# Three instructions moved in the hand-written order of a fused S4D and bilinear-GLU kernel

## The chip, the cores and the metric

The kernel runs on one core of a Trainium2 chip. A core has a matrix engine (TensorE, PE in the profile, with its weight loads listed apart as PEld), a vector engine (VectorE, DVE), a scalar engine (ScalarE, ACT), GpSimd (POOL) and SyncE (SP). Each engine works through its own list of instructions strictly in order, and the engines meet through semaphores. Matrix results stand in PSUM, from which DVE or ACT copies them away; SP and POOL issue the DMAs here. The metric is the device time of one execution in microseconds. A change of about 1% is what the measurement of this kernel can tell from none.

## What is computed

Two branches share one output and are mixed by a gate. Branch A is a state-space convolution: a kernel K of 2048 taps for each of 512 channels is built from complex exponentials, and the input is convolved with it by FFT. Branch B is a bilinear feed-forward layer.

```python
# A: S4D convolution, L = 2048, D = 512, N = 128
P = jnp.exp((A * dt[:, None])[:, :, None] * pos[None, None, :])
K = 2.0 * jnp.einsum("dn,dnl->dl", C, P).real
y = jnp.fft.irfft(jnp.fft.rfft(u_t, L2) * jnp.fft.rfft(K, L2)[None], L2)[:, :, :L]
a = y.transpose(0, 2, 1) + u * D_skip[None, None, :]
# B: bilinear GLU, F = 1792
b = jnp.einsum("bsf,fd->bsd", (x @ w_gate) * (x @ w_up), w_down)
# the mix
g = sigmoid((u * gate_w).sum(-1, keepdims=True))
out = g * a + (1 - g) * b
```

## The kernel before

**Branch B** (`glu`, line 820) holds most of the matrix work. The 14 tiles of F stand in four groups of 3, 3, 4 and 4, and for each group the four chunks of 512 tokens are passed. `hidden` (line 726) forms `pg` and `pu` for one tile of F, each from 12 matmuls of 512 columns: every float32 product is split into a high and a low part and taken as three matmuls. ACT copies `pg` into `h`, DVE multiplies by `pu`, ACT casts the high part `hh`, and DVE subtracts for the low part `hl`. `down` (line 753) multiplies `hh` and `hl` with the down weights and sums over the group in a PSUM bank `y`, one for each 128 tokens. There are two banks `y`, so the third of a chunk waits until the first has been copied away. `evacuate` (line 764) does that: an ACT activation `acc<-y,ngate` scales by 1 - g, and a DMA issued by POOL adds `acc` to the output in memory. `acc` has three buffers.

**Branch A** builds its tables on DVE and ACT. `v_table` (line 1165) makes the table `v` for one of 16 blocks of the state, by an outer product and then twice by squaring: ACT squares the real part into `v` and the imaginary part into `sq`, DVE forms twice the product (`SCALAR_TENSOR_TENSOR v<-v`) and subtracts (`TENSOR_TENSOR v<-v,sq`). The first squaring has 16 columns, the second 8 and reads the first. `k_block` (line 1206) multiplies the tables `x` and `v` on PE into a bank `k`, which ACT and DVE bring into `kt`. Every fourth block a quarter of the channels is complete and goes through the transform: `k_first` (line 1240), then four times `m_second` (line 1325: 32-row matmuls into four banks `k`, copied by ACT into `ev`), `m_product` (line 1351: complex product of the spectra on DVE, `y<-ev`, `ev<-ev`, twice `y<-y,ev`), twice `m_inverse` (line 1382: back into four banks `k`, copied by ACT into `ts`, written to memory `y_d`), and `m_last`. There are four banks `k`.

**The order.** All this is recorded as tasks, numbered as they are added. `Work.plan` (line 357) sets an order for each engine by a planner with estimated durations. Then `Work.run` (line 455) applies a table of numbers, `AHEAD` (line 446): a pair (n, m) takes task n out of its engine's line and puts it directly ahead of task m. After that the instructions are issued in this order, engine by engine; an engine never leaves its order. The lines of the page read L126 for all of them, since one helper, `InOrder`, records every operation; so groups are told apart by the names of their tiles.

```python
for n, other in self.AHEAD:
    line = lines[at[n].engine]
    line.remove(at[n])
    line.insert(line.index(at[other]), at[n])
```

Of the kernel before, what the change touches and what calls it, by code (L numbers as in the profile page):

```python
# [206 lines left out]
class Work:  # L207
# [149 lines left out]
    def plan(self):  # L357
# [95 lines left out]
    )  # L453

# [1163 lines left out]
```

## Time and profile before

| | |
|---|---|
| Median of 3 runs | 584.13 us (579.15, 584.13, 584.96) |
| The profiled execution | 578.89 us, of which the span from first to last instruction is 577.1 us |
| DVE busy | 509.9 us (88%) |
| ACT busy | 400.9 us (69%) |
| POOL busy | 113.6 us (20%) |
| DMA | 136.28 MB moved, mean 236 GB/s |
| Granted TensorE clock | 1.000 of full speed over the span |

Of a timeline's row the columns are: start in us from the span's beginning, duration in us, engine, line, operation, out<-in, shapes, count, and in brackets the idle time of the engine before it with what ended it. Rows of equal instructions that follow each other are merged, with their count behind an x. Ends of matmuls are modelled. An engine's next instruction can start some hundredths of a microsecond before the end of the one ahead of it.

### The profile page before, as it was taken

The numbers are of one execution on the slowest core, as the hardware profiler recorded it, in microseconds if no ns is written. First come the engines' busy times: TensorE is split into PE (matmuls) and PEld (weight loads), VectorE is DVE, ScalarE is ACT, GpSimd is POOL, SyncE is SP. The second block draws the span as 40 slices with busy tenths as digits, with TensorE's granted clock in tenths as the row PEclk, the third lists the DMA queues.
The fourth block names the chain that finished last, engine by engine and source line by source line (L and its number), as shares of the span: only waits on it lengthen the run. The fifth ranks groups of instructions, "written<-read, shape, count | busy, mean of one in ns | idle before, by whom it ended". The sixth has DMA issues, their size and how long they took to land.

```text
span 577.1 us, 14851 instructions
## 1 busy us (share of the span) xinstructions
PE 571.2 (99%) x6006; PEld 435.4 (75%) x6006; DVE 509.9 (88%) x812; ACT 400.9 (69%) x891; POOL 113.6 (20%) x159
## 2 busy tenths in 40 slices
PE   8999999999999999999999999999999999999997
PEld 7777777888886877788677868876878786776775
DVE  6999999999998989999999999997999996247555
ACT  5459888997588499967896775799877534243351
POOL 0003222412010240311122401102333103111011
PEclk9999999999999999999999999999999999999999
DMA  8999969998665798989779857978989349798976
GB/s 277 403 348 371 415 223 348 272 231 241 126 178 141 273 231 186 253 204 285 201 219 245 197 134 246 220 186 210 304 138 297 71 167 255 243 294 235 289 160 127
DMA packets 71687, 136.28 MB, mean 236 GB/s; under 512 B 6852, under 2 KB 35780, under 8 KB 69188
## 3 DMA queue, kind: packets, MB, share of 16 engines
q1 hardware_dynamic: 47668, 87.10, 43.8%
q0 software_dynamic: 23392, 47.98, 39.8%
q8 instruction: 47, 0.77, 0.5%
q10 hardware_dynamic: 560, 0.26, 0.2%
q14 instruction: 20, 0.16, 0.1%
HBM read 80.27 MB, written 55.05 MB: 234 GB/s over the span
## 4 chain that ended last, share of the span: by engine, by line
PE 79%; DVE 13%; ACT 4%; DMA 2%; issue 2%; DVEq 0%
PE y L126 23%; PE pg L126 22%; PE pu L126 22%; PE k L126 12%; DVE v L126 3%; DVE x L126 2%; DMA raw<-in_wts 2%; DVE h L126 1%; DVE y L126 1%; DVE hl L126 1%; DVE m L126 1%; DMA y<-in_xT 1%; ACT ev L126 1%; DVE ev L126 1%; DVE t L126 1%
## 5 line engine op out<-in xcount | busy, mean ns | idle before, releaser
L126 PE MATMUL pg<-xs,whi 128*128 128x512 f32 x448 | 138.6, 390 | 0.5 <-ACT whi L126 0.5
L126 PE MATMUL pu<-xs,whi 128*128 128x512 f32 x448 | 138.1, 389 | 0.0
L126 PEld LDWEIGHTS pg<-xs,whi 128*128 128x128 f32 x448 | 84.0, 188 | 18.3 <-ACT whi L126 0.7
L126 PEld LDWEIGHTS pu<-xs,whi 128*128 128x128 f32 x448 | 84.1, 188 | 17.1
L126 PE MATMUL y<-dhi,hl 128*128 128x512 f32 x224 | 90.3, 403 | 0.3 <-ACT acc L126 0.2
L126 PE MATMUL pg<-xs,wlo 128*128 128x512 f32 x224 | 89.3, 399 | 0.0
L126 PE MATMUL pu<-xs,wlo 128*128 128x512 f32 x224 | 89.0, 397 | 0.0
L126 PE MATMUL y<-dlo,hh 128*128 128x512 f32 x224 | 87.4, 390 | 0.0
L126 PE MATMUL y<-dhi,hh 128*128 128x512 f32 x224 | 87.2, 389 | 0.0
L126 POOL DMA_DIRECT2D out<-acc x44 | 38.7, 938 | 168.7 <-ACT acc L126 168.3
L126 ACT COPY ev<-k 128x512 f32<-128x512 f32 x112 | 59.5, 599 | 14.0 <-PE k L126 11.3
L126 ACT CAST hh<-h 128x512 fp32r<-128x512 f32 x56 | 34.7, 620 | 46.4 <-DVE h L126 46.1
L126 DVE TENSOR_TENSOR h<-pu,h 128x512 f32<-128x512 f32 x56 | 38.5, 687 | 23.2 <-PE pu L126 20.8
L126 ACT ACTIVATE acc<-y,ngate 128x512 f32<-128x512 f32 x62 | 41.9, 688 | 24.0 <-PE y L126 22.2
L126 PEld LDWEIGHTS y<-dhi,hl 128*128 128x128 f32 x224 | 42.0, 187 | 21.5 <-issue 7.8
L126 PEld LDWEIGHTS pg<-xs,wlo 128*128 128x128 f32 x224 | 42.0, 188 | 18.4 <-issue 9.2
L126 PEld LDWEIGHTS pu<-xs,wlo 128*128 128x128 f32 x224 | 42.0, 188 | 15.7 <-issue 6.1
L126 ACT COPY h<-pg 128x512 f32<-128x512 f32 x56 | 33.0, 590 | 28.4 <-PE pg L126 22.5
L126 PEld LDWEIGHTS y<-dhi,hh 128*128 128x128 f32 x224 | 42.1, 188 | 9.0
L126 PEld LDWEIGHTS y<-dlo,hh 128*128 128x128 f32 x224 | 42.1, 188 | 7.8
L126 DVE TENSOR_TENSOR hl<-h,hh 128x512 fp32r<-128x512 f32 x56 | 38.5, 688 | 5.4 <-ACT hh L126 4.8
L126 DVE TENSOR_TENSOR v<-m,v 128x896 f32<-128x896 f32 x32 | 34.1, 1085 | 0.2
(134 smaller groups left out, 961.3 us busy)
## 6 DMA issues: line engine op xcount, KB each, us to landing
xs<-xs_d SPq DMA_DIRECT2D x36, 512.0 KB, 6.2
out<-acc POOLq DMA_DIRECT2D x44, 256.0 KB, 6.5
raw<-in_wts SPq DMA_DIRECT2D x33, 256.0 KB, 4.7
xs_d<-xs SPq DMA_DIRECT2D x16, 512.0 KB, 7.8
su_d<-ev POOLq DMA_DIRECT2D x32, 256.0 KB, 6.1
y_d<-ts SPq DMA_DIRECT2D x28, 256.0 KB, 5.6
in<-su_d POOLq DMA_DIRECT2D x12, 512.0 KB, 8.0
sk_d<-ev SPq DMA_DIRECT2D x6, 1024.0 KB, 3.9
```

The source lines that it names most:

```text
L126: got = getattr(self.engine, name)(*args, **kw)
```

## The change

Three pairs are added to the table. Nothing else is changed: no instruction is added or taken away, and the lists of PE, SP and POOL stay as they were.

```diff
         (2111, 1052), (2112, 2204), (2225, 2204), (2108, 2113), (2110, 2113), (1054, 2114),
+        (939, 1905), (2326, 2178), (1260, 2182),
         (2168, 1223), (2307, 1226), (2320, 1226), (2169, 1227), (2170, 1227),
```

The first pair, (939, 1905), moves the copy of the last `y` of a chunk in the third group on ACT. In the list of before it stands between a copy of `pg` into `h` and a load of an activation table; `t` and `rt` are phases, `x`, `kt` and `v` pieces of the tables of branch A.

```order
L126 COPY h<-pg 128x512
L126 ACTIVATE acc<-y,ngate 128x512
L126 ACT_TABLE_LOAD
L126 ACTIVATE t<-t 128x672
L126 COPY x<-pb 128x64
L126 COPY kt<-k 128x8x2x16
L126 ACTIVATE rt<-rt,fixed 128x672
L126 COPY v<-ri 128x32x4
L126 COPY v<-ri 128x32x7
L126 COPY v<-ri 128x32x4
L126 COPY v<-ri 128x32x7
L126 CAST hh<-h 128x512
```

The same stretch of ACT's list now:

```order
L126 COPY h<-pg 128x512
L126 ACT_TABLE_LOAD
L126 ACTIVATE t<-t 128x672
L126 COPY x<-pb 128x64
L126 COPY kt<-k 128x8x2x16
L126 ACTIVATE rt<-rt,fixed 128x672
L126 COPY v<-ri 128x32x4
L126 COPY v<-ri 128x32x7
L126 COPY v<-ri 128x32x4
L126 COPY v<-ri 128x32x7
L126 CAST hh<-h 128x512
L126 ACTIVATE acc<-y,ngate 128x512
```

The copy into `acc` stands ten instructions later, behind the cast of `h` into `hh` and ahead of the copies of `k` into `ts`. The DMA that adds this `acc` to the output keeps its place in POOL's list and waits for the copy.

The second pair, (2326, 2178), is on DVE, in the last quarter of the kernel, where the last block's `v` is squared beside the spectral product (`y` and `ev`) of the third quarter of the channels.

```order
 L126 TENSOR_TENSOR y<-ev 128x1024
 L126 SCALAR_TENSOR_TENSOR v<-v 128x32x16
-L126 TENSOR_TENSOR ev<-ev 128x2x2x256
-L126 TENSOR_TENSOR v<-v,sq 128x32x16
+L126 TENSOR_TENSOR v<-v,sq 128x32x16
+L126 TENSOR_TENSOR ev<-ev 128x2x2x256
 L126 TENSOR_TENSOR y<-y,ev 128x512
 L126 SCALAR_TENSOR_TENSOR v<-v 128x32x8
```

The end of the first squaring of `v` has changed places with the second half of the product.

The third pair, (1260, 2182), is on ACT at the same time of the program, behind the second squaring of `v`.

```order
 L126 ACTIVATE v<-v 128x32x8
 L126 ACTIVATE sq<-v 128x32x8
-L126 COPY ev<-k 128x2x2x128
-L126 ACTIVATE acc<-y,ngate 128x512 x2
+L126 ACTIVATE acc<-y,ngate 128x512
+L126 COPY ev<-k 128x2x2x128
+L126 ACTIVATE acc<-y,ngate 128x512
 L126 COPY ev<-k 128x2x2x128 x3
 L126 COPY kt<-k 128x8x2x16
```

The first of two copies into `acc` has changed places with the first of four copies of `k` into `ev`.

## The prediction

> **What bounds the kernel now.** I read the page first: busy times and the chain of work that ended last.
>
> ```profile
> span 577.1 us, 14851 instructions
> ...
> PE 571.2 (99%) x6006; PEld 435.4 (75%) x6006; DVE 509.9 (88%) x812; ACT 400.9 (69%) x891; POOL 113.6 (20%) x159
> ...
> PE 79%; DVE 13%; ACT 4%; DMA 2%; issue 2%; DVEq 0%
> ```
>
> PE holds 79% of the chain and is busy for 99% of the span. A move on another engine can therefore only shorten the time where PE stands still for that engine. The second view is the list of waits, PE alone; its columns are the total, the number and the longest, in us.
>
> ```profile
> PE k L126 <- DVE acc L126: 1.1, 1, 1.1
> PE pg L126 <- ACT whi L126: 0.5, 1, 0.5
> PE y L126 <- ACT acc L126: 0.2, 1, 0.2
> ```
>
> That is all PE waits for in this execution: 1.8 us. The first two lie at the start (the warm-up's zeroes and the first weights). The third is a matmul into `y` that waits for ACT to copy an older `y` into `acc`, and this is the operation that two of the three moves shift. So I looked for that wait in the timelines. PE:
>
> ```profile
> 477.87 0.39 PE L126 MATMUL y<-dhi,hh 128*128 128x512 f32 x1
> ...
> 479.02 0.61 PE L126 MATMUL pg<-xs,whi 128*128 128x512 f32 x2
> 479.80 0.50 PE L126 MATMUL y<-dhi,hl 128*128 128x512 f32 x1 [0.16 <-ACT acc L126]
> 480.14 0.40 PE L126 MATMUL y<-dlo,hh 128*128 128x512 f32 x1
> 480.38 0.40 PE L126 MATMUL y<-dhi,hh 128*128 128x512 f32 x1
> 480.70 1.99 PE L126 MATMUL k<-v,x 128*32 128x64 f32 x128
> ...
> 486.94 2.00 PE L126 MATMUL k<-kt,w1k_t 32*128 32x512 f32 x16
> ```
>
> The matmul at 479.80 is the first of the chunk's third `y` and needs the bank of the first `y`, whose last matmul is that at 477.87. ACT and DVE at the same time:
>
> ```profile
> 475.14 0.64 ACT L126 ACTIVATE sq<-v 128x512 f32<-128x512 f32 x1
> 477.79 0.69 ACT L126 ACTIVATE v<-v 128x256 f32<-128x256 f32 x1 [2.01 <-DVE v L126]
> 478.26 0.43 ACT L126 ACTIVATE sq<-v 128x256 f32<-128x256 f32 x1
> 478.59 0.56 ACT L126 COPY ev<-k 128x512 f32<-128x512 f32 x1
> 479.06 1.26 ACT L126 ACTIVATE acc<-y,ngate 128x512 f32<-128x512 f32 x2
> 480.21 1.56 ACT L126 COPY ev<-k 128x512 f32<-128x512 f32 x3
> ```
>
> ```profile
> 475.32 0.68 DVE L126 SCALAR_TENSOR_TENSOR v<-v 128x512 f32<-128x512 f32 x1
> 475.92 1.21 DVE L126 TENSOR_TENSOR ev<-ev 128x1024 f32<-128x1024 f32 x1
> 477.06 0.69 DVE L126 TENSOR_TENSOR v<-v,sq 128x512 f32<-128x512 f32 x1
> ...
> 481.80 1.23 DVE L126 TENSOR_TENSOR y<-ev 128x1024 f32<-128x1024 f32 x1 [1.86 <-ACT ev L126]
> ...
> 486.07 0.26 DVE L126 TENSOR_TENSOR kt<-kt,skip 128x64 f32<-128x64 f32 x1
> ```
>
> ACT waits 2.01 us for DVE's `v<-v,sq` at 477.06, then squares, copies one `ev`, and only at 479.06 begins the `acc` that PE needs. It ends at 479.06 + 0.69 = 479.75 (one `acc` is 688 ns in the page), and PE starts at 479.80.
>
> **Moves two and three, the late `acc`.** What the wait costs: the two `pg` matmuls at 479.02 take 0.61 together and one alone 0.39, so the step from one to the next is 0.61 - 0.39 = 0.22 to 0.23. The next was due at 479.02 + 0.23 + 0.23 = 479.48 and came at 479.80: 0.32 late. The step behind it is 480.14 - 479.80 = 0.34 where 0.23 is usual: 0.11 more. The cost is 0.43 us.
>
> [...] The rows show steps of 0.22 to 0.24 us with nothing waiting, so the sum goes by the rows.
>
> Move two puts `v<-v,sq` at 475.92, in the place of `ev<-ev`. Its `sq` is ready at 475.14 + 0.64 = 475.78, and DVE is free at 475.92, so it doesn't wait. It ends at 476.61; ACT, which started 0.04 after DVE's end before (477.06 + 0.69 = 477.75, then 477.79), squares from 476.65 and is done at about 477.5, 1.14 earlier. `ev<-ev` then runs from 476.52 to 477.73 and the next product starts where `v<-v,sq` ended before. For the rest of DVE the two only change places: cost nothing.
>
> Move three lets `acc` start as soon as ACT is free and the first `y` is ready. How soon that is shows where ACT waited for PE, elsewhere in the trace:
>
> ```profile
> 364.54 0.39 PE L126 MATMUL y<-dhi,hh 128*128 128x512 f32 x1
> ```
>
> ```profile
> 364.97 0.69 ACT L126 ACTIVATE acc<-y,ngate 128x512 f32<-128x512 f32 x1 [0.26 <-PE y L126]
> ```
>
> That is 0.43 after the last matmul's start, so here 477.87 + 0.43 = 478.30. With both moves `acc` runs from 478.30 to 478.99, and PE may go on at 479.04, 0.44 ahead of its due time 479.48. The wait is gone: -0.43 us. The two moves are each enough alone. With move three alone `acc` takes the place of `ev` at 478.59, ends at 479.28, and PE is free at 479.33. With move two alone `ev` comes first, but at about 477.5, and `acc` again starts at 478.30. Their gains do not add.
>
> What pays: the first `ev` copy now starts behind `acc`, at 478.30 + 0.59 = 478.89 in place of 478.59, and ends at about 479.45. Its bank is the first that `k<-v,x` can take, which moves to 480.27: 0.8 to spare. The four `ev` copies end at about 481.5, no later than the 481.77 of before, so DVE's `y<-ev` is no later either. What is late next: `k<-kt` on PE moves from 486.94 to 486.51. It needs DVE's `kt<-kt,skip`, which ends at 486.33 even if DVE gains nothing. That leaves 0.18, so the gain passes here too. Bounds: 0 (another wait takes it up) and -0.43; I take -0.43, since each follower quoted has room.
>
> **Move one.** Its place, on ACT and then on DVE:
>
> ```profile
> 328.92 0.70 ACT L126 ACTIVATE acc<-y,ngate 128x512 f32<-128x512 f32 x1
> ...
> 334.03 0.62 ACT L126 CAST hh<-h 128x512 fp32r<-128x512 f32 x1
> 337.32 0.59 ACT L126 COPY ts<-k 128x512 f32<-128x512 f32 x1 [2.67 <-PE k L126]
> ```
>
> ```profile
> 333.31 0.69 DVE L126 TENSOR_TENSOR h<-pu,h 128x512 f32<-128x512 f32 x1
> ```
>
> All from the table load to the copies into `v` starts up to 0.6 earlier. But `hh` needs DVE's `h`, ready at 333.31 + 0.69 = 334.00, and started at 334.03. So `hh` gains nothing, and the 0.6 becomes idle time ahead of it. `acc` then runs from about 334.55 to 335.25, in the 2.67 us in which ACT waits for PE. PE has no wait within 10 us of this place, so nothing there can be gained: 0. What it might cost is the bank `y` and the store, both 5.6 us later:
>
> ```profile
> 348.82 0.39 PE L126 MATMUL y<-dhi,hl 128*128 128x512 f32 x1
> ```
>
> ```profile
> 356.91 1.72 POOL L126 DMA_DIRECT2D out<-acc  x2 [26.09 <-ACT acc L126]
> ```
>
> The next `y` is asked for at 348.82, 13 us after the copy ends. POOL has been idle for 26 us when it issues its next DMA, so nothing is queued behind the later store. Cost 0; the bounds are 0 and the 3.3 us of the second rival.
>
> **The sum.** 0 - 0.43 = -0.43 us: span 576.7, and 578.46 against the 578.89 of the profiled execution, or -0.07%. The runs shown lie in two places, 579.15 beside the profiled 578.89, and 584.13 and 584.96; the median of three, 584.13, is in the upper. A gain of 0.43 does not move runs from one to the other, so I put the new median at 584.13 - 0.43 = 583.7.
>
> **Rivals.** *No gain.* PE is not the true bound, or a wait behind the place takes the 0.43 back. For it: the 0.18 of `k<-kt`, and DVE's 13% of the chain. Against it: no PE wait is listed behind 479.80. [...] Time: 578.89, median 584.1.
>
> *Slower by the late store.* The `acc` of move one now is sent at about 335.3 and meets the writes of `y_d` and the loads behind them on SP's queue:
>
> ```profile
> 339.36 2.72 SPq L126 DMA_DIRECT2D y_d<-ts  x4
> ...
> 348.17 0.50 SPq L126 DMA_DIRECT2D in<-y_d  x1
> 348.71 1.54 SPq L126 DMA_DIRECT2D xs<-xs_d  x3
> ```
>
> ```profile
> xs<-xs_d SPq DMA_DIRECT2D x4, 512.0 KB, 8.8
> ...
> y_d<-ts SPq DMA_DIRECT2D x4, 256.0 KB, 3.0
> ```
>
> ```profile
> DMA to landing us min/median/max: 4.0/6.3/12.1
> ```
>
> ```profile
> 364.77 0.39 PE L126 MATMUL pg<-xs,wlo 128*128 128x512 f32 x1
> ```
>
> The last of the three rows of landings is that of `acc`. `y_d` lands at about 342.08 + 3.0 = 345.1, 3.1 ahead of `in<-y_d`. The last `xs` lands at about 350.25 + 8.8 = 359.1, 5.7 ahead of PE's use of it. It decides from a delay of 3.1 + 5.7 = 8.8 us. If the store's longest landing, 12.1, came on top in full, PE would wait 12.1 - 8.8 = 3.3 us: 582.2 for the profiled execution and 587.4 for the median. Against it: at the usual 6.3 the store is through before `y_d` is half written.
>
> *Faster by the runs' spread.* If the 5.2 us between the two places where runs lie are waits at one of the three moved instructions, the median falls to 578.5. For it: nothing in the trace, which is of the quicker kind. Against it: three moves of 0.6 us each.
>
> **How the numbers follow.** The forecast has 0.60, no gain 0.25, the late store 0.05, the spread 0.10. The predicted time is 583.7. The range goes from 578.0, the lower place with the gain and 0.5 for the scatter within a place, to 585.8, the highest run and as much again as the two upper runs differ (0.83). About 1% of 584.13 is 5.8 us, what a measurement can tell from none: below 578.3 or above 590. Faster takes half of the spread's case (its 578.5 lies on the edge) and 0.07 for a median that falls to the lower place by chance: 0.12. Slower takes the late store when it is worse than priced, and as much for chance: 0.05. The rest, 0.83, is no change.
>
> **What would show it.** Right: at about 479.5 PE goes from `pg` to `y` without a wait for `acc`, ACT's second squaring starts near 476.6, `acc` near 478.3, and `k<-kt` comes some 0.4 earlier. Move one: `acc` near 334.6, idle time ahead of `hh`, and PE as before up to 365. Wrong: a new PE wait behind 480, or `xs` late at 365.

## The result and the profile after

Beside each other, in 14 executions each:

| kernel | median us | lowest to highest |
|---|---|---|
| before | 582.26 | 578.83 to 585.75 |
| after | 578.77 | 578.17 to 579.61 |

The ratio is 0.9939, with a 95% interval of 0.9916 to 0.9961: 0.6% faster. The whole interval lies below 1, but the step is smaller than the 1% that counts as a change for this kernel, so the two count as the same. The lower ends differ by 0.7 us, the upper ends by 6.1 us. The change has made the time of the quick executions of before the usual one. The forecast was 583.7 us, and no change: the verdict came true, the time lies within the range of 578.0 to 585.8, and the median is 4.9 us off.

The profiled execution of after took 579.12 us, against 578.89 of before, though the median fell by 3.5 us. The profile of before is thus one of its quick executions, and a comparison of the two profiled executions shows no gain. The page of after:

```profile
span 577.3 us, 14851 instructions
...
PE 571.8 (99%) x6006; PEld 436.1 (76%) x6006; DVE 510.3 (88%) x812; ACT 400.8 (69%) x891; POOL 113.4 (20%) x159
...
PE 98%; DMA 1%; ACT 0%; DVE 0%; issue 0%; DVEq 0%
```

The chain that ended last is now PE for 98%, where it was PE for 79%. The list of waits of PE in after (total, number, longest) has only the two of the start left:

```profile
PE k L126 <- DVE acc L126: 1.1, 1, 1.1
PE pg L126 <- ACT whi L126: 0.5, 1, 0.5
```

The place of moves two and three, in the timelines of after (start, duration, both us, then the instruction; the idle time ahead of it in brackets). PE:

```profile
479.65 0.62 PE L126 MATMUL pg<-xs,whi 128*128 128x512 f32 x2
480.11 0.39 PE L126 MATMUL y<-dhi,hl 128*128 128x512 f32 x1
480.33 0.39 PE L126 MATMUL y<-dlo,hh 128*128 128x512 f32 x1
480.56 0.39 PE L126 MATMUL y<-dhi,hh 128*128 128x512 f32 x1
481.03 1.99 PE L126 MATMUL k<-v,x 128*32 128x64 f32 x128
...
487.30 2.00 PE L126 MATMUL k<-kt,w1k_t 32*128 32x512 f32 x16
```

From the pair of `pg` to the first `y` PE takes 480.11 - 479.65 = 0.46 us, where it took 0.78, and from there to the next 0.22, where it took 0.34: 0.44 us gained, and the forecast had 0.43. Behind it, `k<-v,x` starts 0.47 after the matmul ahead of it; in before that step was 0.32. So 0.15 is given back. DVE in after shows why:

```profile
477.08 0.91 DVE L126 TENSOR_TENSOR v<-v,sq 128x512 f32<-128x512 f32 x1
477.87 1.25 DVE L126 TENSOR_TENSOR ev<-ev 128x1024 f32<-128x1024 f32 x1
...
480.23 0.66 DVE L126 TENSOR_TENSOR v<-v,sq 128x256 f32<-128x256 f32 x1
```

The second `v<-v,sq` writes what `k<-v,x` reads and ends at 480.89, while PE was due at 480.56 + 0.32 = 480.88 and began at 481.03. ACT in after, at the place of move one and then at that of move three:

```profile
328.79 0.59 ACT L126 COPY h<-pg 128x512 f32<-128x512 f32 x1 [0.19 <-PE pg L126]
329.39 1.28 ACT L126 ACT_TABLE_LOAD   x1
...
334.38 0.62 ACT L126 CAST hh<-h 128x512 fp32r<-128x512 f32 x1 [0.33 <-DVE h L126]
334.90 0.68 ACT L126 ACTIVATE acc<-y,ngate 128x512 f32<-128x512 f32 x1
337.67 0.59 ACT L126 COPY ts<-k 128x512 f32<-128x512 f32 x1 [2.08 <-PE k L126]
...
478.94 0.69 ACT L126 ACTIVATE acc<-y,ngate 128x512 f32<-128x512 f32 x1
479.52 0.58 ACT L126 COPY ev<-k 128x512 f32<-128x512 f32 x1
```

Both copies into `acc` stand where the prediction put them: the first at 334.90 (334.55 was forecast, and the place as a whole comes 0.35 later here), the second at 478.94, which is 0.71 before the pair of `pg`, as forecast (479.02 - 478.30 = 0.72). The steps are right, then, and yet they sum to 0.3 to 0.4 us where the median fell by 3.5. The rest must come from something that the profile of before does not show as a wait.

### The profile page after: what moved, and what is told of

It reads as the page before. It is cut to its first block, busy times and chain, and to the rows that moved or that the text cites. A ratio compares the mean times of both kernels' runs of the same rounds, so it can differ in the third digit from the quotient of the medians.

```text
span 577.3 us, 14851 instructions
## 1 busy us (share of the span) xinstructions
PE 571.8 (99%) x6006; PEld 436.1 (76%) x6006; DVE 510.3 (88%) x812; ACT 400.8 (69%) x891; POOL 113.4 (20%) x159
## 4 chain that ended last, share of the span: by engine, by line
PE 98%; DMA 1%; ACT 0%; DVE 0%; issue 0%; DVEq 0%
PE y L126 28%; PE pg L126 27%; PE pu L126 27%; PE k L126 15%; DMA y<-in_xT 1%; ACT acc L126 0%; ACT xs L126 0%; DVE kt L126 0%; DVEq L1613 0%; ACT whi L126 0%
```

## The experiments

Two theories stood at the start. **The late store**: `acc` has three buffers, so the copy of move one needs the buffer whose store is the first of POOL's three `out<-acc` just ahead. Where POOL is late, that store lands late, ACT stands still at the copy, and everything behind it on ACT is late; move one takes the copy out of that place. **Moves two and three**: the wait at 479.80 is longer in most executions than in the profiled one, and its removal is the gain. The profile of before allows the first. POOL's timeline of before:

```profile
302.61 1.58 POOL L126 DMA_DIRECT2D out<-ts  x1 [2.60 <-ACT x L126]
310.34 1.56 POOL L126 DMA_DIRECT2D out<-ts  x1 [6.15 <-ACT ev L126]
...
321.37 2.75 POOL L126 DMA_DIRECT2D out<-acc  x3
```

and its transfers in the stretch that holds the first of those three alone (count, KB each, us from issue to landing):

```profile
out<-acc POOLq DMA_DIRECT2D x1, 256.0 KB, 7.4
```

The store lands at 321.37 + 7.4 = 328.8, and ACT's copy starts at 328.92: it made it by 0.15 us, and so left no wait.

**Move one alone, moves two and three alone, before once more, and an earlier store.** The rows left in the table of the change were

```diff
+        (939, 1905),
```

> Only the first pair, (939, 1905), is added to the table of before. Theory S (late store): in most runs of before POOL sends the first of three stores out<-acc some 5 us later than in the profiled run; the copy into acc of move one then waits on ACT for that store to land, because it needs its buffer, and everything behind it on ACT is late. Move one takes exactly this copy out of the way, so this kernel alone runs at 578.5 to 579.7 with a scatter of about 1 us, ratio 0.993 to 0.996. Theory P (the prediction's term): the gain is the 0.43 us of moves two and three alone; then this kernel is like before, 578.8 to 585.8, ratio 1.00.

and, in the second kernel,

```diff
+        (2326, 2178), (1260, 2182),
```

> Only the pairs (2326, 2178) and (1260, 2182) are added. Theory S: the scatter of before stays, 578.4 to 585.5, ratio 0.998 to 1.001. Theory P: all of the gain is here; ratio 0.993 to 0.996 and a scatter of about 1 us.

The third is the kernel before, unchanged, for a second profile:

> The kernel before, unchanged, for a second profile. By its 14 runs it lies above 580 in about four of five executions. Theory S: in such an execution the stores out<-acc on POOL near 321 are some 5 us later, the copy into acc near 329 sits idle ahead of it for 2 to 5 us until a store lands, and PE waits for ACT or DVE within the next 20 us, by together about what the run is over 578.9. Theory P: no such wait, and the excess lies elsewhere.

The fourth leaves the order of before, but POOL sends the store of the first `acc` ahead of the three loads before it in its list:

```diff
+        line = lines["pool"]
+        store = line.index(at[925])
+        line.insert(store - 3, line.pop(store))
```

> ACT's and DVE's order of before, no pair added. On POOL alone the first of the three stores out<-acc is sent ahead of the last three of the loads that stood before it, so it leaves and lands 2 to 6 us earlier. Theory S: the buffer is free in time in every run, and the time is like that of after, 578.5 to 580, with its small scatter. A rival, O (order): what counts is that ACT's own chain behind the copy is 0.6 us shorter, not the store; then this kernel scatters like before, 578.8 to 585.8.

Measured on one chip, before at 580.72 (578.71 to 586.85, 29 executions):

| kernel | median us | lowest to highest | ratio and 95% interval |
|---|---|---|---|
| move one alone | 579.31 | 578.75 to 580.54 | 0.9963, 0.9933 to 0.9994 |
| moves two and three alone | 579.86 | 578.64 to 583.59 | 0.9978, 0.9944 to 1.0012 |
| earlier store, no move | 579.91 | 578.69 to 580.60 | 0.9963, 0.9936 to 0.9991 |

The three intervals overlap, so the medians alone don't tell these kernels apart; the scatter does. Move one alone and the earlier store alone both take away its upper part: of 12 executions each, none lies above 581 us, where 14 of the 29 of before do. Moves two and three alone leave it: 5 of 12 lie above. The second profile of before took 582.89 us and shows the wait itself. First its POOL:

```profile
315.82 1.56 POOL L126 DMA_DIRECT2D out<-ts  x1 [10.84 <-ACT acc L126]
...
326.76 2.75 POOL L126 DMA_DIRECT2D out<-acc  x3
```

Its ACT, from the copy into `h` on:

```profile
328.48 0.59 ACT L126 COPY h<-pg 128x512 f32<-128x512 f32 x1 [0.19 <-PE pg L126]
332.46 0.69 ACT L126 ACTIVATE acc<-y,ngate 128x512 f32<-128x512 f32 x1 [3.40 <-DMA out<-acc]
333.17 1.28 ACT L126 ACT_TABLE_LOAD   x1
334.46 0.77 ACT L126 ACTIVATE t<-t 128x672 f32<-128x672 f32 x1
335.14 0.28 ACT L126 COPY x<-pb 128x64 f32<-128x64 f32 x1
335.27 0.36 ACT L126 COPY kt<-k 128x256 f32<-128x256 f32 x1
```

Its DVE, behind the copies into `kt`:

```profile
335.67 0.42 DVE L126 TENSOR_TENSOR kt<-k,kt 128x256 f32<-128x256 f32 x1 [2.57 <-ACT kt L126]
```

And its PE, at three places:

```profile
337.17 2.04 PE L126 MATMUL k<-y,w3s 32*64 32x128 f32 x122 [1.45 <-DVE kt L126]
...
346.77 2.28 PE L126 MATMUL k<-in,w2s 32*32 32x512 f32 x32
...
483.66 0.50 PE L126 MATMUL y<-dhi,hl 128*128 128x512 f32 x1 [0.68 <-ACT acc L126]
```

PE's weight loads (PEld) in the second of these places:

```profile
346.77 0.31 PEld L126 LDWEIGHTS k<-in,w2s 32*32 32x32 f32 x4 [0.35 <-ACT ev L126]
347.43 0.13 PEld L126 LDWEIGHTS k<-in,w2s 32*32 32x32 f32 x2 [0.35 <-ACT ev L126]
347.91 0.23 PEld L126 LDWEIGHTS k<-in,w2s 32*32 32x32 f32 x26 [0.35 <-ACT ev L126]
```

And the piece of the chain that ended last which stands ahead of ACT's copy (start, length, what):

```profile
326.76 5.68 DMA out<-acc
```

Read down: POOL's store leaves 5.4 us later than in the first profile of before and lands at 332.44; ACT stands still for 3.40 us at the copy until then, and the table load, `t`, `x` and `kt` come behind it; DVE waits 2.57 us for `kt`; PE waits 1.45 us for DVE. At 346.77 a group that takes 1.14 us in the first profile takes 2.28, another 1.1 us. PE's row names no releaser inside the group, but its weight loads do: they stop three times for ACT's copies `ev`, which free the banks `k` and are late like all of ACT's work behind the copy. In all, PE is level with the first profile where `k<-y,w3s` starts (335.27 here, 335.24 there) and 3.0 us behind it at the first `pu` after this group (348.98 here, 345.97 there). The span is 581.1, 4.0 longer than in the first profile of before: 3.0 are this place, and 0.5 more is lost ahead of the `y` at 483.66, where PE waits 0.68 us for `acc` in place of 0.16. The rest is spread over small steps. Moves two and three alone met the same: their profile has the copy waiting 3.20 us and PE 1.26. (Another 1.4 us of that profile is lost in the first 10 us of the kernel, where nothing was moved.)

The profile of the earlier store and that of move one alone have no wait near 335, though POOL was late in that of the earlier store too: it sent the two `acc` stores that were not moved at 327.00, while the moved one, sent at 317.06, had landed after 9.8 us, at 326.9. In that of move one alone this remains on PE:

```profile
481.01 0.50 PE L126 MATMUL y<-dhi,hl 128*128 128x512 f32 x1 [0.73 <-ACT acc L126]
```

This is the wait of moves two and three. With the slow step behind it, it costs about 1.0 us here, against 0.43 in the profile of before: so both theories hold a part, the first the larger. How long this wait is depends on the execution: before itself has 0.16 us of it in one profile and 0.68 in the other.

**Which of moves two and three does it, and a store made late by force.** Two kernels have move one with one of the others:

```diff
+        (939, 1905), (1260, 2182),
```

> After without its second pair (no exchange on DVE). The prediction held move three to be enough alone: then this kernel is like after, 578.2 to 579.6, and PE goes to the third y near 480 without a wait. Rival: in the usual execution DVE comes later to v<-v,sq than in the profile of before, ACT's squaring follows it and acc with it, so PE waits 0.3 to 1.0 us there; median 0.3 to 0.8 above that of after.

```diff
+        (939, 1905), (2326, 2178),
```

> After without its third pair (the copy of k into ev stays ahead of acc on ACT). The prediction held move two to be enough alone: then like after, 578.2 to 579.6, no wait near 480. Rival: one copy of 0.47 us ahead of acc is too much in the usual execution, where DVE is late; PE waits 0.1 to 0.5 us, and the median is 0.1 to 0.5 above that of after.

Two more delay POOL by a row of small memsets ahead of the first `out<-acc`, one in before and the same in after:

```diff
+    idle = const.tile([P, 1], F32, name="idle")
+    store = work.tasks[925]
+    send = store.fn
+
+    def late_store():
+        for _ in range(84):
+            pool_q.memset(idle, 0.0)
+        send()
+
+    store.fn = late_store
```

> Before, with 84 small memsets (about 2.8 us by those at the start) on POOL directly ahead of the first of the three stores out<-acc. Theory S (late store): ACT's copy into acc waits that much longer; in executions that already waited the time rises by nearly 2.8, in the others by what is over the 1 us they had to spare; median 583 to 586, and the lowest above 580. Rival O (order alone): POOL's work there is hidden, and the kernel is like before, with lowest runs at 578.8.

> After, with the same 84 memsets on POOL at the same place. Theory S: the moved copy stands near 334.9 and the store lands near 333 plus 2.8, so the copy waits at most about 1 us, inside the 2 us in which ACT waits for PE; the time is like that of after, 578.2 to 580. Rival O: the delay costs the same in both orders.

Measured, before at 581.67 (578.59 to 584.66, 29 executions):

| kernel | median us | lowest to highest | ratio and 95% interval |
|---|---|---|---|
| moves one and three | 579.12 | 578.53 to 580.63 | 0.9961, 0.9940 to 0.9982 |
| moves one and two | 578.52 | 578.08 to 580.50 | 0.9953, 0.9930 to 0.9977 |
| before, store delayed | 588.86 | 587.75 to 589.62 | 1.0123, 1.0080 to 1.0165 |
| after, store delayed | 579.29 | 578.64 to 580.74, and one at 1995.63 | 0.9966, 0.9937 to 0.9995 |

The one execution of 1995.63 us stands alone among all of this study, and nothing in these runs explains it.

With moves one and three PE still waits for `acc`:

```profile
480.84 0.50 PE L126 MATMUL y<-dhi,hl 128*128 128x512 f32 x1 [0.21 <-ACT acc L126]
```

With moves one and two there is no such wait. ACT in that kernel:

```profile
477.58 0.59 ACT L126 COPY ev<-k 128x512 f32<-128x512 f32 x1
478.37 1.38 ACT L126 ACTIVATE acc<-y,ngate 128x512 f32<-128x512 f32 x2 [0.20 <-PE y L126]
```

ACT has copied `ev` and now waits 0.20 us for PE's `y`: beside move one, move two without three brings ACT there early enough, and move three has nothing left to give. The medians agree: that of moves one and three lies 0.6 us higher on the same chip.

The delay was meant to be 2.8 us and came to 13.1: the 84 memsets took 156 ns each, where those at the kernel's start, by which they were sized, took 36. The test is the stronger for it. POOL in before with the delay:

```profile
320.57 13.10 POOL L126 MEMSET idle<- 128x1 f32 x84
334.12 2.70 POOL L126 DMA_DIRECT2D out<-acc  x3 [0.45 <-issue]
```

PE in the same profile:

```profile
342.89 3.70 PE L126 MATMUL k<-y,w3s 32*64 32x128 f32 x122 [7.11 <-DVE kt L126]
```

PE waits 7.11 us, and the median lies 10.0 us above the quick 578.89, in which there was no such wait (and 7.2 above the median of before, whose executions hold shorter waits of this kind). The other 2.9 us go, by the estimate of the last section, to a granted clock of 0.50 behind the wait. In after the store leaves at 333.48, as late, and ACT waits for it at the copy, in its new place:

```profile
337.88 0.69 ACT L126 ACTIVATE acc<-y,ngate 128x512 f32<-128x512 f32 x1 [3.48 <-DMA out<-acc]
338.47 0.58 ACT L126 COPY ts<-k 128x512 f32<-128x512 f32 x1
```

The list of PE's waits of that kernel has nothing but the 1.1 us of the start, and its span is 577.1. One group alone is longer, by 0.4 us, and ACT's copies `ts`, which free the banks `k`, run until 339.41 + 1.59 = 341.00 there:

```profile
340.64 1.54 PE L126 MATMUL k<-in,w2s 32*32 32x512 f32 x32
```

It takes 1.14 us in the other profiles of after. A store some 13 us later costs before 10 us against its quick execution and costs after about 0.4: this settles what move one does.

**What makes the store late, and the two best once more.** In every profile so far POOL sends a first `out<-ts` between 301 and 305 and a second several us behind it, and in between, from 304.5 to 306.3, SP begins to send four loads of `xs`. The table has these profiles by how long before the first load of `xs` the first `out<-ts` leaves:

| profile | first `out<-ts` | ahead of `xs` | lands after | second | between |
|---|---|---|---|---|---|
| after, store delayed | 301.40 | 3.12 | 7.6 | 309.37 | 8.0 |
| before, store delayed | 302.23 | 2.64 | 7.3 | 309.85 | 7.6 |
| before | 302.61 | 2.15 | 7.4 | 310.34 | 7.7 |
| after, second profile | 302.84 | 1.98 | 7.3 | 310.45 | 7.6 |
| move one alone | 303.38 | 1.75 | 9.1 | 312.75 | 9.4 |
| moves one and two | 303.06 | 1.67 | 9.6 | 312.96 | 9.9 |
| moves two and three alone | 304.69 | 1.58 | 10.9 | 315.87 | 11.2 |
| moves one and two, second profile | 303.08 | 1.54 | 9.5 | 312.94 | 9.9 |
| before, second profile | 303.40 | 1.40 | 12.1 | 315.82 | 12.4 |
| after | 303.74 | 1.37 | 11.0 | 315.06 | 11.3 |
| earlier store, no move | 303.63 | 1.19 | 11.3 | 315.24 | 11.6 |
| moves one and three | 303.43 | 1.14 | 10.8 | 314.53 | 11.1 |

The second store leaves 0.3 to 0.4 us after the first has landed, in all of them. Where the first leaves 1.98 us or more ahead of `xs`, it lands in 7.3 to 7.6 us; where it leaves 1.75 us or less ahead, in 9.1 to 12.1.

So, between the two profiles of before, 0.8 us at the first `out<-ts` becomes 5.4 us at the `acc` stores. The test delays POOL in before ahead of the first `out<-ts` alone, with 28 such memsets (`work.idle` makes them):

```diff
+        first = line[line.index(at[925]) - 6]
+        send = first.fn
+
+        def late_store():
+            self.idle()
+            send()
+
+        first.fn = late_store
```

> Before, with 28 small memsets (156 ns each in the last two runs with memsets, 4.4 us, of which POOL has 2.6 to spare) on POOL ahead of the store out<-ts near 303, the first of the queue of which the late store is the end. Theory A (collision): when this store is sent some 1 to 2 us later than in the quick profile, it meets the four loads of xs that SP sends at 304.8, takes 11 to 12 us in place of 7.7, and everything behind it on POOL is late in every run; out<-acc is sent at 325 or later, ACT's copy into acc waits, and the time is 581.5 to 585 with no run below 580.5. Rival: the lateness has another source, further back or random; then the time scatters from 579 to 585 as in before.

> After, unchanged, beside the next kernel on the same chip. If move three (acc ahead of one copy into ev) is worth nothing once moves one and two stand, its median lies within 0.4 us of that kernel's, 578.3 to 579.2; if it is worth the 0.1 to 0.5 us of the earlier rival, this one is the faster by that.

> Moves one and two without move three, again. Nothing-more theory: 578.3 to 579.2, within 0.4 us of after on the same chip. The first measurement of it had a median 0.25 below that of after, on another occasion; if it beats after for good, it does so here by 0.2 us or more.

Measured, before at 580.65 (578.54 to 586.84, 29 executions):

| kernel | median us | lowest to highest | ratio and 95% interval |
|---|---|---|---|
| before, `out<-ts` delayed | 584.31 | 583.59 to 586.65 | 1.0051, 1.0013 to 1.0089 |
| after | 578.71 | 578.06 to 579.95 | 0.9947, 0.9914 to 0.9981 |
| moves one and two | 578.96 | 578.01 to 579.83 | 0.9932, 0.9902 to 0.9962 |

POOL in before with the delay:

```profile
305.13 1.58 POOL L126 DMA_DIRECT2D out<-ts  x1 [0.73 <-DVE x L126]
317.67 1.56 POOL L126 DMA_DIRECT2D out<-ts  x1 [10.96 <-ACT sq L126]
...
327.25 2.77 POOL L126 DMA_DIRECT2D out<-acc  x3
```

With the first `out<-ts` 2.5 us later than in the first profile of before, it leaves 0.5 us behind the first load of `xs` and lands after 12.2 us. The second comes 7.3 us later, and all executions lie at 583.59 or above, in the upper half of what before does by itself; three of the ten are above the 585 that was expected. That a later POOL there lengthens the whole is shown by this. That it is the loads of `xs` which slow the first store is argued from the times alone. Why POOL comes to that first `out<-ts` up to 2 us earlier or later against `xs` from one execution to the next is open: its load of `in<-sk_d` ahead of it already starts between 298.8 and 301.2, after 2.9 to 4.1 us that the trace puts down to issue.

The profile of after shows the same late store without its price. Its POOL:

```profile
326.00 2.75 POOL L126 DMA_DIRECT2D out<-acc  x3
```

The first of these took 6.1 us to land, at 332.1. In its old place, behind the copy into `h` that ends at 329.38, the copy into `acc` would have stood still for 2.7 us. In its new place, at 334.90, it finds the buffer free.

In four profiles with the wait, the copy's wait and PE's wait can be set side by side:

| profile | ACT at `acc` | PE at `k<-y,w3s` | difference |
|---|---|---|---|
| moves two and three alone | 3.20 | 1.26 | 1.94 |
| before, second profile | 3.40 | 1.45 | 1.95 |
| before, `out<-ts` delayed | 5.53 | 3.58 | 1.95 |
| before, store delayed | 9.07 | 7.11 | 1.96 |

The place of move one has 1.95 us of room, and what goes beyond it reaches PE in full. Move two with or without three gives 578.71 and 578.96 beside each other: no difference that can be told. No kernel tried is faster than after by more than the scatter. In the three comparisons, 44 of 87 executions of before lie above 581 us, and, with those of the result, none of the 74 of the kernels that have move one and no delay. A fourth buffer for `acc` was not tried.

## Why the prediction was right and wrong

**Right by luck: the verdict and the range.** "No change" came true, and 578.77 lies between 578.0 and 585.8, but only because the range was drawn down to the quick executions. The forecast itself was a gain of 0.43 us from moves two and three and nothing from move one; the runs have 3.5 us. Where the profiles show the waits, that of move one costs 3.0 us and that of moves two and three 0.4 to 1.0.

**Right, with their size**: the wait at 479.80 goes, by 0.44 us where 0.43 was forecast; with all three moves both copies into `acc` start at the forecast time; the copy of move one goes into ACT's idle time, and costs nothing. The second rival, the late store that collides with `y_d` and `xs`, is refuted: after with that store at 338.92 has no wait in PE's list behind it. Its room was smaller than the prediction had it: the first `in<-y_d` is sent at 346.93, not 348.17, so 1.8 us behind the landing of `y_d` in place of 3.1.

**Wrong: "PE has no wait within 10 us of this place, so nothing there can be gained: 0."** That holds for the profiled execution of before and not for about half of the others. The copy had 0.15 us to spare to a landing that came at 328.8 in one profile of before and at 332.4 in the other, and the prediction looked at what follows the copy, never at what the copy itself needs: a free buffer, hence a landed store. Its term was 0. In the second profile of before, the place costs 3.0 us.

**Wrong: "a gain of 0.43 does not move runs from one to the other."** True of the 0.43, but the conclusion that the new median is in the upper place fell with move one's term. Nor are there two places: the 14 executions of the result fill the stretch from 578.8 to 585.8. The three times shown (579.15, 584.13, 584.96) said that something in this kernel varies by 5 us, and the profiled 578.89 that the profile is of the kind in which it doesn't happen. The third rival said just this and what it would give, 578.5; the runs gave 578.77. It was held at 0.10 because "nothing in the trace" spoke for it. But such a trace can't speak for it, since it is the kind without the wait. What could have spoken were the 0.15 us of room, which stood in the trace unread.

**Mis-sized: moves two and three.** 0.43 was right for the profiled execution. Move one alone, against after, shows some 0.6 us (579.31 and 578.71, though from two comparisons on different chips), and its profile about 1.0 at that place. Also wrong: "the two moves are each enough alone". Move two is, beside move one; move three leaves a wait of 0.21 us there. And "for the rest of DVE the two only change places: cost nothing" is wrong: from the start of the first `SCALAR_TENSOR_TENSOR v<-v` to that of the second DVE takes 479.76 - 476.48 = 3.28 us in after, where it took 478.26 - 475.32 = 2.94. The second `v<-v,sq` comes 0.34 us later by that, which is more than the 0.15 by which it held `k<-v,x`.

**Mis-named: what is late next.** `k<-kt` was given as the follower with the least room, 0.18. What held PE was `k<-v,x`, by 0.15 in this profile, 0.18 in the second of after, and by nothing with moves one and two, where DVE comes earlier relative to PE. Move three isn't the reason: in after with the delayed store, which has it, DVE comes as early, and `k<-v,x` is not held. The first `v<-v` starts 1.15 to 1.20 us ahead of PE's `k<-in,w2s` near 476 in the three profiles without the hold, and 0.34 to 0.39 ahead in the two with it. What makes DVE earlier or later is open.

## What to carry to other kernels

Where the executions of a kernel scatter by more than the change can bring, find out first which kind the profile is of, and look in it for waits that were just avoided: a copy that starts 0.15 us after its buffer's store has landed is as much a suspect as one that waited. For each instruction on a path with little room, compare the landing of every transfer that it needs with its start, not only the releaser that the trace names. An instruction that needs a transfer belongs behind the work that doesn't, above all on an engine whose later work feeds the bound.

## What the runs showed of the hardware

In the two longest waits of PE in these profiles, 3.58 and 7.11 us, the granted clock fell to 0.50. In before with `out<-ts` delayed, PE waited 3.58 us until 339.10; the stretches of that profile (start and end, length, busy time of PE, PEld, DVE, ACT and POOL with counts, granted clock, DMA share, GB/s):

```profile
335.00:338.86 3.86, 0.52 (x7) 0.20 (x6) 1.26 (x3) 3.83 (x9) 0.84 (x1) 1.00 0.87 131
338.86:342.28 3.42, 3.18 (x117) 3.21 (x122) 2.26 (x4) 1.22 (x4) 0.00 (x0) 0.50 0.05 10
342.28:346.00 3.72, 3.72 (x33) 2.81 (x20) 3.72 (x5) 2.80 (x6) 0.00 (x0) 1.00 0.50 144
```

The clock is 0.50 for 3.4 us, and `k<-y,w3s` takes 3.50 us in place of 2.04. After the 7.11 us wait of the other delayed kernel it was 0.50 for 10.2 us, from 338.5 to 348.7; PE worked from 342.89 on, so 5.8 us of its work ran at half the clock and cost some 2.9 us more, an estimate that takes half of the 5.8. After the 1.45 us in the second profile of before it stayed at 1.00. The clock fell at 338.86 in the shorter of the two waits, 3.34 us after the end of PE's last matmul (335.08 + 0.44 = 335.52), and at 338.5 in the longer, 2.7 us after it (335.34 + 0.44 = 335.78). How long PE has to stand still for this, and what sets the length of the slow stretch, the runs don't show. The clock goes with the top of before's scatter: of its 87 executions in the three comparisons, the 15 above 584 us all have a mean granted clock of 0.993 to 0.997, and the 43 below 581 us all have 0.998 or more. In the two delayed kernels the late store cost PE its wait, 3.58 and 7.11 us, and then the clock: 3.50 - 2.04 = 1.46 us on `k<-y,w3s` in the one, the 2.9 us of the estimate in the other.

The first `out<-ts`, a DMA that adds to the output, took 7.3 us from issue to landing in the second profile of after and 12.2 in before with the delay, where it left behind the first of the four loads of `xs`. And 21 memsets of 128x1 on POOL at the start, each of another column, took 0.76 us in all, or 36 ns a step; the 84 put ahead of the store, all of one column, took 156 ns a step. No run tells what makes the difference.
